# One weight block fewer converted during attention, longer first segments in the first layer, and two changes in the second layer's sums

## The chip, the cores and the metric

The kernel runs on one core of a Trainium2 chip. The metric is the device time of one execution in microseconds, as the median of several runs.

## The reference

Causal attention with a decay (4 batches of 8 heads, 576 positions, 64 per head), and behind it two feed-forward layers on 2304 tokens of 512 elements:

```python
log_f = np.log(np.clip(f, 0.0001, 1.0))
cum = np.cumsum(log_f, axis=-1)
scores = scale * q @ k.T + (cum[:, :, :, None] - cum[:, :, None, :])   # causal
attn = softmax(scores) @ v                    # -> x [2304, 512]
h = x @ w_in                                  # w_in [512, 2048]
x = (h * np.cos(h)) @ w_out                   # w_out [2048, 512]
g, val = x @ w_gate, x @ w_val                # [512, 1536] each
out = (g / (1 + np.exp(-g)) * val) @ w_out2   # w_out2 [1536, 512]
```

## The kernel before

All weights arrive as 64-bit integers that hold the bits of a double; the kernel turns them into fp32 itself, and makes each fp32 product from a high and a low part, so that one product of a 128-wide block with a chunk of 384 tokens is 12 matmuls of 128x384.

**Weight blocks.** There are 68 blocks of 128x512: 32 of `w_in` and `w_out` of the first layer (called i0 to i15 and o0 to o15 here), 36 of the second layer. `w_load` (L149) loads a raw block through SP into one of two `wraw` buffers. `w_step` converts it in steps: 1 is an Abs on ACT (L165), 2 to 5 are four instructions on DVE (L167 to L173), 6 rounds to the high part (POOL, L115, in attention, ACT, L187, later) and 7 is POOL's subtraction for the low part (L112). Blocks of the second layer go instead to `w_member`: POOL sums (L206), ACT highs, POOL lows, and SP stores to DRAM (L220). The first SA = 16 blocks in the order of a list are converted during attention, with buffers of its own; the rest (the next stage) during the first layer. The list alternates in and out blocks, i0, o0, i1, o1 and so on.

**Attention** runs 16 head pairs through a table of operations (`SCH`, "operation@offset"; w1 to w7 are the steps of a block, wd its load, xo the store of a pair's output x1 to DRAM, L539). `op` and `act` carry them out.

**First layer.** Six chunks of 384 tokens times 16 blocks make 96 steps. A step issues in1 (12 matmuls with w_in, L250, into h), and on ACT n (L661), on DVE r (L663), on ACT the sine (L665), on DVE h (L667), on ACT gh (L669) and on DVE gl (L112); two steps later comes out1 (12 matmuls with w_out, L684; L687 for a segment's last block). Chunks 0 and 1 are cut into two segments each: `SEG` runs blocks 0 to JS - 1 of both, then the rest of both, the sum between being kept in a part in DRAM (L697). ACT, DVE and the others work in the written order; `ORD1` is the order within a step, and each "w" in it may take a substep (2 to 5) of a conversion. `WQ` says how many do:

```python
left = WQ[wpos[0] >= SB and i % 2] if i >= WS else 0     # WQ = (3, 2), SB = 32, WS = 2
```

So three of the four substeps of a block in each step until 32 blocks are done, then three and two in turn. With substep 5 the next block's Abs is issued, and the load of the block after (`w_load(n + RWB2)`). Each later chunk's x is loaded (L264) some steps ahead and split by POOL (xh L115, xl L112). A `gate` (L141) is a one-element write on DVE that holds the load of chunk 1's x until the last pair's attention is done.

**Second layer.** Sums and differences of 2x2 blocks cut eight products to seven. `in2` runs 18 units of seven products (12 matmuls, L872); DVE combines them (L749) in tiles u (six buffers, p1, u2 and u3 of a unit), and silu times value goes to tiles g (two buffers). Three dummy allocations of u ahead of it set which u buffer comes first. `out2` runs 18 sets (t) of products (L961); DVE's sums (`g_sums`) and splits (`g_split`, high on ACT L743, low on DVE L112) of set t + 1 are issued between the products of set t, at places given by `GSUMS` (`GSUM0` for t = 0), `HAT` and `LATG`.

Of the kernel before, what the change touches and what calls it, by code (L numbers as in the profile page):

```python
# [9 lines left out]
F32 = mybir.dt.float32  # L10
# [10 lines left out]
NPAIR = NH // 2  # L21
# [5 lines left out]
CH = 384  # L27
NC = NT // CH
HT = NT // 2
SA = 16  # L30
LAG = 2
PB = 4
RWB = 3
# [10 lines left out]

CPD = ("10", "11")
SCH = "M21@2 ld@0 M00@2 rt@3 M01@2 T40@3 M30@2 T30@3 re@4 C20@3 rc@3 C40@3 C30@3 T10@3 M31@2 w6@4 C10@3 w1@3 T11@3 C11@3 T00@3 C00@3 T01@3 E20@2 C01@3 S4@2 S1@2 V1@4 rf@4 E21@2 w2@3 E30@2 w3@3 w4@3 E31@2 q3@1 M40@2 M10@2 wd@2 E00@2 E01@2 q0@0 M11@2 rd@3 V0@4 S2@1 lv@3 E40@2 S0@1 w5@3 E10@2 xk@3 xo@5 E11@2 q1@0 qb@0 S3@1 T20@2 N1@4 ra@2 N0@4 rb@2 M20@1 w7@4 q2@0"
JS = 8
NCH = 96
NPASS, NQ, NST = 3, 6, 2
NIT = NPASS * CH // 128  # L50
# [1 line left out]
PO = (1, 6, 2, 7, 5, 4, 3)  # L52
PO2 = (1, 5, 6, 2, 7, 3, 4)
HAT = (2, 3, 4, 5, 6, 7, 8)
LAT = (4, 5, 5, 6, 7, 8, 9)
LATG = (3, 4, 5, 6, 7, 8, 9)
# [2 lines left out]
POS_IN = {1: 0, 2: 1, 5: 2, 6: 3, 7: 4, 3: 5, 4: 6}  # L59
POS_OUT = {2: 0, 3: 1, 5: 2, 6: 3, 7: 4, 4: 5, 1: 6}  # L60
GSUMS = ((0, 0), (1, 1), (2, 2), (3, 3))
GSUM0 = ((2, 0), (3, 1), (4, 2), (6, 3))
SEAM = {1: (2, 3), 6: (3, 4), 5: (4, 5), 2: (5, 6), 7: (6, 7), 3: (7, 8), 4: (8, 9)}
ORD1 = "0c152cw64cowwc"
WQ = (3, 2)
NS = 2
WS = 2
# [27 lines left out]
def body(ctx: ExitStack, tc: tile.TileContext, qk, v, f, w_in, w_out, w_gate, w_val, w_out2, mask_c, ident_c, sel_c, out):  # L95
# [24 lines left out]
    SB = 2 * J1  # L120
    srcs = {"i": w_in, "o": w_out, "g": w_gate, "v": w_val, "p": w_out2}
    order = []
    for j in range(SA // 2):
        order += [("i", j), ("o", j)]
# [10 lines left out]
    held, now = [0], [0]  # L135
# [413 lines left out]

    def op(o, i):  # L550

        if not 0 <= i < NPAIR + (o[0] == "w"):
            return
        if i == 0:
            o = {"M40": "M10", "M10": "M11", "M11": "M40"}.get(o, o)
        elif i == 1:
            o = {"S2": "S3", "S0": "S2", "S3": "S0"}.get(o, o)
        if i in (0, 1, NPAIR - 1):
            o = {"rt": "T40", "T40": "T30", "T30": "rt", "rc": "C40", "C40": "C30", "C30": "rc"}.get(o, o)
        if (o, i) in BEHIND:  # L560
            return
        for a in AHEAD.get((o, i), ()):
            act(*a)
        act(o, i)

    AHEAD = {("M21", 1): (("ra", 0), ("rb", 0)), ("M00", 1): (("E20", 1),), ("C40", 0): (("E21", 1),),
             ("w6", NPAIR): [(f"w{k}", NPAIR) for k in range(2, 6)]}
    BEHIND = {a for b in AHEAD.values() for a in b}

    def act(o, i):  # L570
# [129 lines left out]
    wpos = [SA, 2]  # L700
# [27 lines left out]
    def x_tile(b):  # L728
        xid[b], X[b] = slot_tile([128, 2, CH], F32, "xb")
# [34 lines left out]
    for i in range(NCH + LAG):  # L764
        if i < NCH:
            g, j = steps[i]
            c, a, b = SEG[g]
            if j == max(a, b - 5):
                part[g] = pp.tile([128, KD, CH], F32, tag="part", name="part")
                if a:  # L770
                    SP.dma_start(out=part[g], in_=x2[c])
            if j == J1 - 7 and c + 1 not in loaded or c == 0 and j == 2 and 1 not in loaded:
                loaded.add(c + 1)
                load_chunk(c + 1, later=True)
            if i == 0:
                for n in range(RWB2):
                    w_load(SA + n)
            if i == WS:
                w_step(SA, 1)
            left = WQ[wpos[0] >= SB and i % 2] if i >= WS else 0  # L780
            now[0] = i
            for k in ORD1:
                if k in "01234":
                    in1(c, j, int(k))
                elif k in "56" and i:
                    in1(SEG[steps[i - 1][0]][0], steps[i - 1][1], int(k))
                elif k == "w" and left:
                    left -= 1
                    w_next()
                elif k == "o" and i >= LAG:  # L790
                    out1(*steps[i - LAG])
                elif k == "c" and small and small[0][0] <= i:
                    small.pop(0)[1]()
            if xsplit and i >= XS:
                split_x(*xsplit.pop(0))
            if i == NCH - 1:
                in1(c, j, 5)
                in1(c, j, 6)
        else:
            out1(*steps[i - LAG])  # L800
        if i == TCL:
            assert wpos[0] >= len(order) and not small and not xsplit, (wpos, len(small))
            rctx.close()
            cp[0] = ctx.enter_context(tc.tile_pool(name="cmb", bufs=1, side=SIDE_R, reuse_waits="tile"))
        if i >= LAG and steps[i - LAG][0] == last:
            j = steps[i - LAG][1]
            free += [2 * j, 2 * j + 1]
            if j == 1:
                for e in range(4):
                    x_tile(e)  # L810
                    x_read(e, 0)
            elif j == 3:
                for e in range(4, 7):
                    x_tile(e)
                jobs += [(u, k) for u in range(4) for k in PO]
            while jobs and free:
                u_read(*jobs.pop(0))
        if TCL < i <= TCL + 4:
            x_sums()[i - TCL - 1]()
        if TCL < i <= TCL + 7:  # L820
            x_split(PO[i - TCL - 1], 0)
            x_split(PO[i - TCL - 1], 1)
# [4 lines left out]
    wk = ctx.enter_context(tc.tile_pool(name="wk", bufs=1, reuse_waits="tile"))  # L827
    ps = ctx.enter_context(tc.tile_pool(name="ps", bufs=1, space=PSUM, reuse_waits="tile"))
    for t in "cd":
        ps.tile([128, 2, 512], F32, tag=t, name=t)  # L830
    for _ in range(3):
        wk.tile([128, 2, CH], F32, tag="u", name="u", bufs=6)

    def parts(i):
        return ((0, 0), (1, 0), (0, 1))
# [19 lines left out]
    def in2(p, q, after, final):  # L855

        pa, pb = (ps.tile([128, 2, 512], F32, tag=t, name=t) for t in "ab")
        ct = ps.tile([128, 2, 512], F32, tag="c", name="c")
        a, b, c = (t[:, :, :CH] for t in (pa, pb, ct))
        acc = {1: (a, 1, 0), 2: (a, 0, 1), 6: (b, 1, 0), 7: (b, 0, 0), 4: (b, 0, 1), 5: (c, 1, 0), 3: (c, 0, 1)}  # L860
        p1, u2, u3 = (wk.tile([128, 2, CH], F32, tag="u", name=n, bufs=6) for n in ("p1", "u2", "u3"))
        g = wk.tile([128, 4, CH], F32, tag="g", name="g", bufs=2)
        for i in PO:
            o, s, e = acc[i]
            for mem in range(2):
                n = 0
                for x, y in ((0, 0), (1, 0), (0, 1)):
                    for kt in range(2):
                        d, r = o[:, mem], cmb[i][:, y, kt]
                        if final and not mem and n == 0 and i in (5, 6):  # L870
                            d, r = (ct if i == 5 else pb)[:, 0], cmb[i][:, 0].rearrange("p k t -> p (k t)")[:, :512]
                        PE.matmul(d, lhsT=wu[q, i][1][:, mem, x, 128 * kt:128 * kt + 128], rhs=r,  # L872
                                  start=bool(s and n == 0), stop=(n == 5), skip_group_check=True)
                        n += 1
            if i == 1:
                ACT.copy(out=p1, in_=a)
            elif i == 6:
                tt(u2, b, p1, add)
            elif i == 2:
                silu(DVE, a, g, p, q, 0)  # L880
            elif i == 7:
                tt(u3, b, p1, add)
            elif i == 5:
                tt(u3, c, u3, add)
                if final:
                    at(3, silu, DVE, u3, g, p, q, 3)
                else:
                    silu(POOL, u3, g, p, q, 3)
            elif i == 4:
                tt(p1, b, p1, add)  # L890
                if final:
                    at(3, silu, DVE, p1, g, p, q, 2)
                else:
                    silu(POOL, p1, g, p, q, 2)
            else:
                tt(u2, c, u2, add)
                at(1, silu, POOL, u2, g, p, q, 1)
            after(i)
# [14 lines left out]
    def g_split(t, i, k):  # L913
        g = [x[1] for x in GT[t]]
        s1, s2, s4 = (sums[e][1] for e in range(3))
        (low_c if k else high_c)(i, {1: g[0], 6: s2, 2: g[2], 7: g[1], 5: s1, 4: g[3], 3: s4}[i])
        if i == 4 and k:
            free.extend(x[0] for x in GT.pop(t))
# [67 lines left out]
        while jobs and len(free) > n:  # L986
            u_read(*jobs.pop(0))

    def splits(fn, lat, po=PO):
        for i, h, d in zip(po, HAT, lat):  # L990
            at(h, fn, i, 0)
            at(d, fn, i, 1)

# [14 lines left out]
    for st in range(NST):  # L1008
        for p in range(NPASS):
            final = st == NST - 1 and p == NPASS - 1  # L1010
            for q in range(NQS * st, NQS * st + NQS):
                k = q - NQS * st
# [23 lines left out]
    for t in range(NIT):  # L1036
        if t + 1 < NIT:
            for d, n in GSUMS if t else GSUM0:
                at(d, g_sums, t + 1, n)
            splits(lambda i, k, t=t: g_split(t + 1, i, k), LATG, PO2)  # L1040
        if t + 2 < NIT:
            at(2, g_load, t + 2)
        out2(t, lambda i: step())
# [58 lines left out]
```

## Time and profile before

| | us |
|---|---|
| median of 3 runs | 976.17 (974.88 to 976.98) |
| profiled execution | 975.54 |
| its span in the trace | 973.8 |
| PE busy | 963.0 (99% of the span) |
| DVE, ACT, POOL busy | 730.8, 506.0, 465.3 |
| mean granted TensorE clock | 0.998 |

The span runs from the first to the last instruction; the profiled execution is 1.74 us longer. Times within the trace are counted from the span's start.

### The profile page before, as it was taken

Reading aid. Unit: us, or ns where it says so; the run is one execution under the profiler, and the core shown is the slowest. Engines: PE = TensorE matmul, PEld = TensorE weight load, DVE = VectorE, ACT = ScalarE, POOL = GpSimd, SP = SyncE. Lnnn points to the kernel's source line nnn. Section 1 sums busy time; section 2 is a strip of 40 time slices with the busy share of each in tenths; the row PEclk is TensorE's granted clock in tenths of the full one; section 3 lists DMA queues with packets and bytes.
Section 4 is the critical chain, followed back from the end, with each engine's and each line's share of the span. In section 5 each row is a group of like instructions: output and inputs, shape, how many; then the busy total and the mean of one; then the engine's idle time right before and its main releaser. Section 6 shows DMA issues by size and latency. Waiting matters only on the chain.

```text
span 973.8 us, 17222 instructions
## 1 busy us (share of the span) xinstructions
PE 963.0 (99%) x6106; PEld 909.3 (93%) x6106; DVE 730.8 (75%) x1309; ACT 506.0 (52%) x1106; POOL 465.3 (48%) x494
## 2 busy tenths in 40 slices
PE   8999999999999999999999999999999999999998
PEld 5778787899999999999999999999999999888888
DVE  6988887787788877779775635766768585898884
ACT  7888887465545655646555432323224132454552
POOL 7787875332257678686582005445445455100000
PEclk9999999999999999999999999999999999999999
DMA  6666656333467868768757773325941329953431
GB/s 190 213 214 193 218 171 190 131 119 108 152 195 250 248 195 285 223 215 283 248 186 244 254 267 109 113 68 200 334 129 51 114 63 382 353 179 126 135 108 44
DMA packets 108981, 182.55 MB, mean 187 GB/s; under 512 B 8912, under 2 KB 72800, under 8 KB 108896
## 3 DMA queue, kind: packets, MB, share of 16 engines
q1 hardware_dynamic: 108896, 181.46, 57.2%
q8 instruction: 48, 0.79, 0.3%
q14 instruction: 37, 0.30, 0.1%
HBM read 118.43 MB, written 62.99 MB: 186 GB/s over the span
## 4 chain that ended last, share of the span: by engine, by line
PE 92%; DMA 3%; ACT 2%; DVE 2%; issue 1%; POOL 0%; DVEq 0%; ACTq 0%; POOLq 0%; SPq 0%
PE h L250 19%; PE t L684 18%; PE b L872 11%; PE c L872 8%; PE a L872 7%; PE b L961 5%; PE t L525 4%; PE t L474 4%; PE a L961 3%; PE sB L405 2%; PE c L961 2%; PE d L961 2%; PE t L687 2%; PE sA L405 2%; PE sA L413 2%; DMA wraw<-in_w_in_dram 1%
## 5 line engine op out<-in xcount | busy, mean ns | idle before, releaser
L250 PE MATMUL h<-xh,w 128*128 128x384 f32 x768 | 148.9, 334 | 0.0
L684 PE MATMUL t<-gh,w 128*128 128x384 f32 x704 | 138.4, 338 | 3.1 <-ACT gh L669 3.0
L250 PEld LDWEIGHTS h<-xh,w 128*128 128x128 f32 x768 | 134.4, 188 | 0.2 <-issue 0.2
L840 POOL TENSOR_TENSOR s<-u,s 128x384 f32<-128x384 f32 x35 | 39.7, 1136 | 190.6 <-ACT s L839 184.1
L684 PEld LDWEIGHTS t<-gh,w 128*128 128x128 f32 x704 | 124.0, 189 | 4.9 <-ACT gh L669 4.0
L872 PE MATMUL b<-c,wu 128*128 128x384 f32 x648 | 121.3, 334 | 0.3 <-DVE u L749 0.3
L663 DVE SCALAR_TENSOR_TENSOR r<-h,n 128x384 f32<-128x384 f32 x96 | 53.3, 555 | 89.6 <-ACT n L661 89.0
L872 PEld LDWEIGHTS b<-c,wu 128*128 128x128 f32 x648 | 113.0, 188 | 0.7 <-DVE u L749 0.6
L661 ACT ACTIVATE n<-h 128x384 int32<-128x384 f32 x96 | 47.1, 490 | 119.3 <-PE h L250 119.0
L250 PE MATMUL h<-xl,w 128*128 128x384 f32 x384 | 82.3, 334 | 0.0
L872 PE MATMUL c<-c,wu 128*128 128x384 f32 x432 | 80.7, 334 | 0.0
L872 PE MATMUL a<-c,wu 128*128 128x384 f32 x432 | 80.7, 334 | 0.0
L684 PE MATMUL t<-gl,w 128*128 128x384 f32 x352 | 75.5, 335 | 0.0
L872 PEld LDWEIGHTS c<-c,wu 128*128 128x128 f32 x432 | 75.4, 188 | 0.0
L872 PEld LDWEIGHTS a<-c,wu 128*128 128x128 f32 x432 | 75.4, 188 | 0.0
L112 POOL TENSOR_TENSOR w<-ta,w 128x512 fp32r<-128x512 f32 x32 | 45.1, 1409 | 56.2 <-ACT w L187 28.3
L436 ACT ACTIVATE P<-P,mx 128x384 f32<-128x384 f32 (+3 forms) x128 | 70.3, 550 | 1.3 <-DVE mx L428 1.2
L250 PEld LDWEIGHTS h<-xl,w 128*128 128x128 f32 x384 | 67.9, 188 | 0.2 <-issue 0.2
L173 DVE SCALAR_TENSOR_TENSOR ta<-wraw,ta 128x512 int32<-128x512 int32 x68 | 66.4, 976 | 0.5
L665 ACT ACTIVATE r<-r,hpi 128x384 f32<-128x384 f32 x96 | 59.6, 620 | 12.7 <-DVE r L663 12.0
L165 ACT ACTIVATE ta<-wraw 128x512 f32<-128x512 f32 x68 | 46.2, 679 | 38.2 <-DMA wraw<-in_w_out_dram 13.1
L684 PEld LDWEIGHTS t<-gl,w 128*128 128x128 f32 x352 | 62.8, 189 | 0.0
(148 smaller groups left out, 2066.6 us busy)
## 6 DMA issues: line engine op xcount, KB each, us to landing
wu<-wu SPq DMA_DIRECT2D x63, 512.0 KB, 4.5
wraw<-in_w_out_dram SPq DMA_DIRECT2D x28, 512.0 KB, 4.2
wu<-hi SPq DMA_DIRECT2D x54, 256.0 KB, 3.9
gd<-g SPq DMA_DIRECT2D x72, 192.0 KB, 2.3
gt<-gd SPq DMA_DIRECT2D x36, 384.0 KB, 4.6
raw<-in_qk_dram SPq DMA_DIRECT2D x16, 576.0 KB, 5.3
wu<-sums SPq DMA_DIRECT2D x36, 256.0 KB, 4.6
xb<-x SPq DMA_DIRECT2D x24, 384.0 KB, 7.6
```

Source lines behind the costliest of these rows:

```text
L112: eng.tensor_tensor(out=o, in0=a, in1=b.bitcast(F32), op=ALU.subtract)
L165: ACT.activation(out=ta.bitcast(F32), in_=hi32, func=AF.Abs)
L173: DVE.scalar_tensor_tensor(out=ta, in0=hi, scalar=-(1 << 30), in1=ta, op0=ALU.bitwise_and, op1=ALU.bitwise_or)
L250: PE.matmul(ps, lhsT=w[:, a, 128 * kk:128 * kk + 128], rhs=b[:, kk], start=(n == 0), stop=(n == 3 * KD - 1))
L436: ACT.activation(out=o, in_=o, func=AF.Exp, scale=-1.0, bias=mxt[p % 8][:, t:t + 1], accum_out=smt[p // 2 % 3][:, c:c + 1])
L661: ACT.activation(out=n, in_=h, func=AF.Copy, scale=INV2PI, bias=0.25)
L663: DVE.scalar_tensor_tensor(out=r, in0=h, scalar=INV2PI, in1=n, op0=ALU.mult, op1=ALU.subtract)
L665: ACT.activation(out=r, in_=r, func=AF.Sin, bias=hpi, scale=float(2 * np.pi))
L684: PE.matmul(acc[m][:, :CH], lhsT=wo[:, q, 128 * m:128 * m + 128], rhs=x, start=(j == a and n == 0), stop=False)
L840: e.tensor_tensor(out=s, in0=C[:, 0], in1=s, op=ALU.mult)
L872: PE.matmul(d, lhsT=wu[q, i][1][:, mem, x, 128 * kt:128 * kt + 128], rhs=r, start=bool(s and n == 0), stop=(n == 5), skip_group_check=True)
L961: PE.matmul(ot[:, :w], lhsT=cmb[i][:, x, q], rhs=m[:, 256 * y:256 * y + w], start=(i in (1, 5) and n == 0), stop=(n == len(ops) - 1), skip ...
```

## The change

Four things. SA becomes 15: the attention's table converts one block less, so the extra w operations behind the last pair go, and the list runs ..., i7, and then i8, o7, i9, o8 and on. JS becomes 9: the first segments of chunks 0 and 1 have nine blocks, the second ones seven. The last 12 blocks are converted at three substeps a step again. In the second layer the first unit's u2 and u3 share one g buffer, the dummy allocations go, and in out2 the sums and splits that are issued with t = 0 come one product later.

```diff
--- before.py
+++ after.py
@@ -27,7 +27,7 @@
 CH = 384
 NC = NT // CH
 HT = NT // 2
-SA = 16
+SA = 15
 LAG = 2
 PB = 4
 RWB = 3
@@ -44,7 +44,7 @@
 
...
-JS = 8
+JS = 9
 NCH = 96
 NPASS, NQ, NST = 3, 6, 2
 NIT = NPASS * CH // 128
@@ -59,7 +59,8 @@
 POS_IN = {1: 0, 2: 1, 5: 2, 6: 3, 7: 4, 3: 5, 4: 6}
 POS_OUT = {2: 0, 3: 1, 5: 2, 6: 3, 7: 4, 4: 5, 1: 6}
 GSUMS = ((0, 0), (1, 1), (2, 2), (3, 3))
-GSUM0 = ((2, 0), (3, 1), (4, 2), (6, 3))
+GSUM0 = ((3, 0), (4, 1), (5, 2), (6, 3))
+HAT0, LAT0 = (3, 4, 5, 6, 7, 8, 8), (4, 5, 6, 7, 8, 9, 9)
 SEAM = {1: (2, 3), 6: (3, 4), 5: (4, 5), 2: (5, 6), 7: (6, 7), 3: (7, 8), 4: (8, 9)}
 ORD1 = "0c152cw64cowwc"
 WQ = (3, 2)
@@ -549,7 +550,7 @@
 
     def op(o, i):
 
-        if not 0 <= i < NPAIR + (o[0] == "w"):
+        if not 0 <= i < NPAIR:
             return
         if i == 0:
             o = {"M40": "M10", "M10": "M11", "M11": "M40"}.get(o, o)
@@ -563,8 +564,7 @@
             act(*a)
         act(o, i)
 
-    AHEAD = {("M21", 1): (("ra", 0), ("rb", 0)), ("M00", 1): (("E20", 1),), ("C40", 0): (("E21", 1),),
-             ("w6", NPAIR): [(f"w{k}", NPAIR) for k in range(2, 6)]}
+    AHEAD = {("M21", 1): (("ra", 0), ("rb", 0)), ("M00", 1): (("E20", 1),), ("C40", 0): (("E21", 1),)}
     BEHIND = {a for b in AHEAD.values() for a in b}
 
     def act(o, i):
@@ -777,7 +777,7 @@
                     w_load(SA + n)
             if i == WS:
                 w_step(SA, 1)
-            left = WQ[wpos[0] >= SB and i % 2] if i >= WS else 0
+            left = WQ[SB <= wpos[0] < SB + 24 and i % 2] if i >= WS else 0
             now[0] = i
             for k in ORD1:
                 if k in "01234":
@@ -828,8 +828,6 @@
     ps = ctx.enter_context(tc.tile_pool(name="ps", bufs=1, space=PSUM, reuse_waits="tile"))
     for t in "cd":
         ps.tile([128, 2, 512], F32, tag=t, name=t)
-    for _ in range(3):
-        wk.tile([128, 2, CH], F32, tag="u", name="u", bufs=6)
 
     def parts(i):
         return ((0, 0), (1, 0), (0, 1))
@@ -858,7 +856,12 @@
         ct = ps.tile([128, 2, 512], F32, tag="c", name="c")
         a, b, c = (t[:, :, :CH] for t in (pa, pb, ct))
         acc = {1: (a, 1, 0), 2: (a, 0, 1), 6: (b, 1, 0), 7: (b, 0, 0), 4: (b, 0, 1), 5: (c, 1, 0), 3: (c, 0, 1)}
-        p1, u2, u3 = (wk.tile([128, 2, CH], F32, tag="u", name=n, bufs=6) for n in ("p1", "u2", "u3"))
+        p1 = wk.tile([128, 2, CH], F32, tag="u", name="p1", bufs=6)
+        if now[0]:
+            u2, u3 = (wk.tile([128, 2, CH], F32, tag="u", name=n, bufs=6) for n in ("u2", "u3"))
+        else:
+            u = wk.tile([128, 4, CH], F32, tag="g", name="g", bufs=2)
+            u2, u3 = u[:, :2], u[:, 2:]
         g = wk.tile([128, 4, CH], F32, tag="g", name="g", bufs=2)
         for i in PO:
             o, s, e = acc[i]
@@ -986,8 +989,8 @@
         while jobs and len(free) > n:
             u_read(*jobs.pop(0))
 
-    def splits(fn, lat, po=PO):
-        for i, h, d in zip(po, HAT, lat):
+    def splits(fn, lat, po=PO, hat=HAT):
+        for i, h, d in zip(po, hat, lat):
             at(h, fn, i, 0)
             at(d, fn, i, 1)
 
@@ -1037,7 +1040,7 @@
         if t + 1 < NIT:
             for d, n in GSUMS if t else GSUM0:
                 at(d, g_sums, t + 1, n)
-            splits(lambda i, k, t=t: g_split(t + 1, i, k), LATG, PO2)
+            splits(lambda i, k, t=t: g_split(t + 1, i, k), *((LATG, PO2) if t else (LAT0, PO2, HAT0)))
         if t + 2 < NIT:
             at(2, g_load, t + 2)
         out2(t, lambda i: step())
```

SP, at the end of attention (x1 stores of the last pairs, raw loads wraw, and xl, the load of chunk 1's x). Before:

```order
L539 DMA x1_60<-xp_2574 128x576
L539 DMA x1_60<-xp_2602 128x576
L149 DMA wraw_2642<-in_w_in_dram 128x512
L149 DMA wraw_2644<-in_w_in_dram 128x512
L264 DMA xl_2687<-x1_60 128x4x384
```

And in the changed kernel:

```order
L540 DMA x1_60<-xp_2572 128x576
L150 DMA wraw_2631<-in_w_in_dram 128x512
L150 DMA wraw_2633<-in_w_out_dram 128x512
L540 DMA x1_60<-xp_2598 128x576
L265 DMA xl_2676<-x1_60 128x4x384
```

The two raw loads moved ahead of the last x1 store.

POOL, at the same place (w13, w14 and so on are blocks, rounded and then subtracted; xh and xl the splits of a chunk). Before:

```order
L112 TENSOR_TENSOR w13_2519<-ta_2405,w13_2519 128x512
L115 TENSOR_SCALAR w14_2580<-ta_2522 128x512
L112 TENSOR_TENSOR w14_2580<-ta_2522,w14_2580 128x512
L115 TENSOR_SCALAR w15_2610<-ta_2582 128x512
L112 TENSOR_TENSOR w15_2610<-ta_2582,w15_2610 128x512
L115 TENSOR_SCALAR xh_2688<-xl_2687 128x384
L112 TENSOR_TENSOR xl_2687<-xl_2687,xh_2688 128x384
```

And in the changed kernel:

```order
L113 TENSOR_TENSOR w13_2519<-ta_2405,w13_2519 128x512
L116 TENSOR_SCALAR w14_2578<-ta_2522 128x512
L113 TENSOR_TENSOR w14_2578<-ta_2522,w14_2578 128x512
L116 TENSOR_SCALAR xh_2677<-xl_2676 128x384
L113 TENSOR_TENSOR xl_2676<-xl_2676,xh_2677 128x384
```

The pair for w15 is gone from here, and the subtraction of w14 is the last of the attention's blocks.

DVE, in out2 with t = 0 (g and u the results of this set, gs and gt sums for the next set, c their low parts). Before:

```order
L749 TENSOR_TENSOR g_9515<-a_9511,g_9515 128x256
L749 TENSOR_TENSOR gt0_9171<-gt31_9170,gt0_9171 128x768
L112 TENSOR_TENSOR c1_9579<-gt31_9170,c1_9579 128x768
L749 TENSOR_TENSOR u_9619<-b_9512,u_9516 128x512
L749 TENSOR_TENSOR g_9515<-u_9619 128x256
```

And in the changed kernel:

```order
L749 TENSOR_TENSOR g_9511<-a_9507,g_9511 128x256
L749 TENSOR_TENSOR gs28_9163<-gt0_9167,gt2_9169 128x768
L749 TENSOR_TENSOR u_9611<-b_9508,u_9512 128x512
L749 TENSOR_TENSOR g_9511<-u_9611 128x256
L749 TENSOR_TENSOR gt0_9167<-gt31_9166,gt0_9167 128x768
L113 TENSOR_TENSOR c1_9597<-gt31_9166,c1_9597 128x768
```

u and the g that is made of it moved ahead of gt0 and of the low part c1.

## Rows read from the trace of the kernel before

**Rows 1.** The page, part 1: busy time, share and instructions of each engine.

```profile
PE 963.0 (99%) x6106; PEld 909.3 (93%) x6106; DVE 730.8 (75%) x1309; ACT 506.0 (52%) x1106; POOL 465.3 (48%) x494
```

**Rows 2.** Waits of PE: line and releaser, us in total, times, longest.

```profile
PE t L684 <- ACT gh L669: 3.0, 3, 2.3
...
PE b L961 <- DVE u L749: 0.4, 1, 0.4
```

**Rows 3.** Chain at the end of attention: start, duration (us), what.

```profile
176.19 3.71 DMA wraw<-in_w_in_dram
...
185.35 2.08 PE h L250 x12
```

**Rows 4.** Timeline there: start, us, engine, line, instruction, idle before.

```profile
168.75 1.28 POOL L112 TENSOR_TENSOR w<-ta,w 128x512 fp32r<-128x512 f32 x1
...
176.93 1.55 PE L250 MATMUL h<-xh,w 128*128 128x384 f32 x8
...
181.44 2.93 PE L684 MATMUL t<-gh,w 128*128 128x384 f32 x8 [2.27 <-ACT gh L669]
...
185.19 1.55 PE L250 MATMUL h<-xh,w 128*128 128x384 f32 x8
```

**Rows 5.** Windows, PE alone: length, busy (instructions), granted clock, DMA share, GB/s.

```profile
179.20:181.40 2.20, 0.00 (x0) 1.00 0.95 345
181.40:183.00 1.60, 1.56 (x5) 0.52 0.87 325
```

**Rows 6.** DMA issues: engine, operation, count, KB each, median us to landing.

```profile
x<-xp SPq DMA_DIRECT2D x16, 288.0 KB, 2.1
```

**Rows 7.** Timeline of the first steps of the first layer.

```profile
202.80 1.29 POOL L112 TENSOR_TENSOR w<-ta,w 128x512 fp32r<-128x512 f32 x1 [1.29 <-ACT w L187]
```

**Rows 8.** Timeline from the first to the second layer.

```profile
574.19 2.24 PE L872 MATMUL a<-c,wu 128*128 128x384 f32 x12
...
579.84 0.96 DVE L749 TENSOR_TENSOR u<-b,p 128x768 f32<-128x768 f32 x1 [4.89 <-DMA x<-part]
...
583.07 2.24 PE L872 MATMUL c<-c,wu 128*128 128x384 f32 x12
```

**Rows 9.** Timeline of the second unit's g.

```profile
593.98 1.02 POOL L841 TENSOR_TENSOR g<-u,s 128x384 f32<-128x384 f32 x1
...
596.87 0.56 DVE L841 TENSOR_TENSOR g<-a,s 128x384 f32<-128x384 f32 x1
```

**Rows 10.** Timeline of out2, t = 0.

```profile
847.54 2.26 PE L961 MATMUL c<-wu,c 128*128 128x512 f32 x12
...
852.43 0.86 PE L961 MATMUL a<-wu,c 128*128 128x512 f32 x3
```

**Rows 11.** Windows of out2: length, busy of PE, PEld, DVE, ACT, POOL, clock, DMA.

```profile
855.00:955.00 100.00, 100.00 (x573) 87.76 (x572) 87.59 (x119) 52.27 (x82) 0.00 (x0) 1.00 0.41 129
```

**Rows 12.** Timeline where chunk 3's x meets the conversions.

```profile
350.18 0.51 POOL L115 TENSOR_SCALAR xh<-xl 128x384 fp32r<-128x384 f32 x1 [4.77 <-DMA xl<-x]
...
369.78 0.67 ACT L165 ACTIVATE ta<-wraw 128x512 f32<-128x512 f32 x1 [5.31 <-DMA wraw<-in_w_val_dram]
```

**Rows 13.** Timeline of PE, where groups start at these two places.

```profile
368.56 1.55 PE L250 MATMUL h<-xh,w 128*128 128x384 f32 x8
...
384.06 1.55 PE L684 MATMUL t<-gh,w 128*128 128x384 f32 x8
...
436.06 1.55 PE L250 MATMUL h<-xh,w 128*128 128x384 f32 x8
...
449.39 1.55 PE L250 MATMUL h<-xh,w 128*128 128x384 f32 x8
```

**Rows 14.** Windows of the first layer, columns as in the windows of out2.

```profile
181.00:270.00 89.00, 88.56 (x502) 88.56 (x503) 72.76 (x136) 50.85 (x102) 30.93 (x24) 0.98 0.38 124
...
475.00:520.00 45.00, 45.00 (x262) 45.00 (x261) 32.35 (x56) 25.03 (x54) 33.91 (x34) 1.00 0.68 220
```

**Rows 15.** L173 from 300 to 500 us: ns min/median/max, first and last start.

```profile
L173 DVE SCALAR_TENSOR_TENSOR ta<-wraw,ta x29: 674/682/1669, 306.9 to 494.3; 128x512 int32<-128x512 int32 x29
```

## Prediction

> **What bounds the kernel now.** The page comes first: PE is busy 963.0 us of a span of 973.8 us, 99%, and no other engine passes 75% [rows 1]. So the end moves only by what PE loses: 10.8 us stand idle, and stretches at a lower clock add to that. The waits of PE are then read: ACT's gh (L669) holds it three times, 3.0 us in all, the longest 2.3 us, and DVE's u (L749) once in the last part, 0.4 us [rows 2]. The rest of the waits lies in the attention, in products that the change leaves in their order. Then the chain of waits and the timeline are read around each of these places. What PE loses at one is the start of a later product less the start of an earlier one, less 2.08 us for each group of twelve matmuls between them, so that slow groups count too. (Twelve matmuls take 2.08 us where nothing disturbs them [rows 3], a step of the first layer two such groups, 4.16 us.)
>
> **Seam 1, attention to first layer.** Two weight loads start at 176.19 us, when POOL has done its subtraction for the 16th block, whose buffer they need; they land 3.71 us later, at 179.90 us, and Abs, n and gh follow on ACT, so that PE starts at 181.44 us after 2.27 us of waiting [rows 3, 4]. The granted clock was still 1.00 while the engine stood idle, and 0.52 behind the gap: TensorE ran at 1.2 in place of 2.4 GHz [rows 5]. Together: the product of step 3 starts at 185.19 us; two groups after 176.93 us would be 176.93 + 2 x 2.08 = 181.09 us. **The place costs 4.10 us**, more than the waits' table shows.
>
> With 15 blocks converted in attention, the raw load of the first block of the next stage waits for the 15th block's subtraction, which ended at 168.75 + 1.28 = 170.03 us [rows 4]: 6.1 us earlier. The loads land at about 170.05 + 3.71 = 173.8 us. PE wants gh at 176.93 + 2.08 = 179.01 us, and from the landing to PE's start 181.44 - 179.90 = 1.54 us went by, so a landing behind 177.5 us would cost something. That leaves 3.7 us of cover; if it is gone, all 4.10 us come back.
>
> What is late next: the x1 store of the last pair now stands on SP behind the two weight loads, and DVE's gate (L141) writes where the attention's last output lay, so that it waits for that store, and h and gh stand behind it. If that store moves only when both loads have landed, and then takes the 2.1 us that an x1 store takes in the median from issue to landing [rows 6], the gate opens at 173.8 + 2.1 = 175.9 us. With the same 1.54 us for h and gh behind it that is about 177.4 us, against 179.0 us. I take the seam as gone, -4.10 us; the bounds are -4.10 and 0.
>
> Four blocks now must be ready that were not among the first: i8, o7, i9 and o8. The fourth block of this stage was subtracted by 202.80 + 1.29 = 204.09 us before [rows 7], so by about 200.0 us now. The in1 of step 3 started at 185.19 us [rows 4], the out1 of step 2 one group later, and the out1 of step 8 six steps of 4.16 us behind that, at 212.2 us; now 4.1 us earlier, at 208.1 us: 8 us to spare. That a segment is nine blocks long rather than eight moves one x2 store by a step, and no wait of PE stands there. Zero.
>
> **Seam 2, first to second layer.** DVE's u waits 4.89 us for the store of the part, since it writes where the part was, and PE behind it starts late. Its fifth group begins at 583.07 us [rows 8], where 574.19 + 4 x 2.08 = 582.51 us was due: **0.56 us**. In a g buffer, u2 waits for no store, and only for PE's product. What it may cost: the second unit's g now takes the buffer that POOL reads last for the first unit, ending at 593.98 + 1.02 = 595.00 us; DVE writes that g at 596.87 us [rows 9], 1.9 us later. Zero, and up to the full 0.56 us back if this cover goes. I take -0.56 us.
>
> **Seam 3, first product set of the last part.** DVE's u comes behind gt and c low, and PE waits 0.4 us for it [rows 2]; its next product but one starts at 852.43 us where 847.54 + 2 x 2.10 = 851.74 us was due [rows 10]: **0.69 us**. (2.10 us for a group here, as it reads 2.26 us where one of the layer before reads 2.24 us [rows 8].) In the new order u stands ahead of gt and c low. An instruction of 768 columns takes 0.96 us on DVE [rows 8], so u comes up to 1.9 us sooner, against 0.4 us of wait. The sums and splits move one product later, and DVE in the 100 us behind is busy 87.59 us [rows 11], so 12 us are left to make that up. -0.69 us; bounds -0.69 and +0.7 (the same wait one product later).
>
> **The middle of the first layer.** At two places a chunk's load meets the conversions. POOL waits 4.77 us for the x [rows 12] and then splits it, with sums between; SP's stores of the sums, which come late, queue in front of the next raw load; the Abs of that block waits 5.31 us [rows 12], and PE for gh behind it. From 368.56 to 384.06 us stand seven groups, 14.56 us, so 0.94 us are lost; from 436.06 to 449.39 us six, 12.48 us, so 0.85 us [rows 13]. **Together 1.79 us.** The two waits for gh left over in the table are 3.0 - 2.3 = 0.7 us [rows 2], some 0.4 us at each, so that an Abs that waits less than about 5.31 - 0.4 = 4.9 us costs PE nothing.
>
> Now the conversions come one block, that is 1.6 steps of 4.16 us at 2.5 of 4 substeps a step, later against these loads, and POOL's order shows the four splits of the fourth chunk spread over sums, where before two pairs stood together. Worked through by hand with the durations of [rows 12], the longest wait of an Abs there becomes some 3.3 us: no loss. In the last chunk loaded, where the last 12 blocks run at three substeps a step again, I get about 4 us, close to the 4.9. I take one such place as left, +0.9 us; bounds 0 and 1.8 us (two).
>
> **The pace of the last 12 blocks.** They take 16 steps in place of 19.2. Where three substeps a step ran before, DVE was busy 72.76 of 89 us, or 3.40 of the 4.16 us of a step; where 2.5 ran late in the layer, 32.35 of 45 us [rows 14]. PE lost nothing in either beyond the seam's end. But in the first of these stretches POOL worked 30.93 of 89 us, in the second 33.91 of 45 us, and beside POOL's sums DVE is slower: from 300 us on L173 takes 674 ns at the least and 1669 ns at the most [rows 14, 15]. The Trainium skill (SBUF — State Buffer, Who interferes with whom) says that a VectorE instruction with two SBUF inputs and a GpSimd instruction take turns under an exclusive lock, so that one waits for the other's whole instruction. The maximum above agrees with it, but the median is 682 ns [rows 15], near the least, so it is seldom met; met in each step it would make the last rival below true. By the rows I take zero.
>
> **The sum.** On the profiled run of 975.54 us: 975.54 - 4.10 - 0.56 - 0.69 - 1.79 + 0.9 = 969.3 us. The median of the runs, 976.17 us, stands 0.63 us above the profiled run, so 969.9 us is what the median should be.
>
> **The rivals.**
> *The middle gets worse.* The faster pace makes the Abs of the last chunk wait longer, and two to four more places of 0.9 us appear. For it: every place in this layer has only some tenths of cover, and SP's queue is in order. Against it: 475 to 520 us shows no loss with POOL at 75%. Time: 969.9 + 0.9 x 2 to 0.9 x 4 = 971.7 to 973.5 us, say 972.6 us.
> *The wait of seam 1 only moves.* The change does not do there what it says: the last x1 store comes too late for the gate, or the loads wait for something else. For it: that store now stands behind two loads of half a megabyte each, and the DMA engines were 95% busy between 179.2 and 181.4 us [rows 5]. Against it: 1.6 us to spare by the sum above. As the clock fell after one gap of 2.2 us, an equal gap gives the 4.10 us back: 974.0 us, up to 974.9 us with no gain in the middle.
> *Slower.* With the last 12 blocks at three a step, DVE becomes the bound. Its 3.40 us, times 1.1 for longer instructions, are 3.74 us, and 0.42 us are left. If one instruction in each step is held for a whole POOL subtraction of 1.29 us [rows 7], that is 5.03 us, 0.87 us too long, over 16 steps 13.9 us: 969.9 + 13.9 = 983.8 us. It is slower than before from 6.3 us over 16 steps, 0.4 us a step. Against it: 181 to 270 us ran at this pace with no such loss.
>
> **How the numbers follow.** The forecast has 0.54 (its own range 968.6 to 971.2 us, from the bounds of the middle and seam 3), the worse middle 0.17, the moved wait 0.14, slower 0.07, and 0.08 is for what goes better, down to 968.4 us (the middle gone whole gives 969.0 us, and 968.4 us if the next median stands no higher than this profiled run). The range 968.4 to 973.6 us leaves out most of the moved wait and the slow case. What can be told from no change is about 0.2%, 1.95 us: faster is below 974.2 us, slower above 978.1 us. Half of the moved wait and 0.03 of the worse middle fall within that: faster 0.54 + 0.08 + 0.14 + 0.07 = 0.83, same 0.10, slower 0.07.
>
> **What would show it.** In the profile after, PE should wait nowhere for gh at about 180 us and the granted clock stay at 1.00 there; the first wraw loads should issue at 170 us, the Abs start by 177 us. No wait for u should stand at the two later seams, the last part's u starting right behind PE's product b. In the middle one group or none should show 2.3 us. A loss between steps 74 and 80, or PE waits for n or gl there, would be the second or the fourth case, and a clock of 0.5 near 180 us the third.

## The result and the profile after

The changed kernel takes 981.29 us in the median (979.80 to 984.86, six runs), the kernel before 975.58 us: ratio 1.0061, 95% interval 1.0040 to 1.0082. It is slower by 0.6%; 969.9 us was forecast. Its profiled execution took 981.45 us, with a span of 979.7 us. (The runs before the prediction, with a median of 976.17 us, are among the six of before.)

The three seams went as forecast. The timeline of the changed kernel at each of them, columns as in [rows 4]:

```profile
169.29 0.34 SPq L150 DMA_DIRECT2D wraw<-in_w_in_dram  x1
...
174.69 0.65 ACT L166 ACTIVATE ta<-wraw 128x512 f32<-128x512 f32 x1
...
175.14 0.14 DVE L142 CAST xl<-gs 1x1 fp32r<-1x1 f32 x1 [0.54 <-DMA x<-xp]
...
176.96 1.55 PE L251 MATMUL h<-xh,w 128*128 128x384 f32 x8
...
181.12 1.55 PE L251 MATMUL h<-xh,w 128*128 128x384 f32 x8
...
580.12 2.24 PE L875 MATMUL a<-c,wu 128*128 128x384 f32 x12
...
588.44 1.72 PE L875 MATMUL c<-c,wu 128*128 128x384 f32 x9
...
852.83 2.26 PE L964 MATMUL c<-wu,c 128*128 128x512 f32 x12
...
857.03 2.26 PE L964 MATMUL a<-wu,c 128*128 128x512 f32 x12
...
867.53 2.26 PE L964 MATMUL c<-wu,c 128*128 128x512 f32 x12
...
869.99 2.37 PE L964 MATMUL b<-wu,c 128*128 128x512 f32 x12 [0.20 <-DVE u L749]
```

At seam 1 the loads issue at 169.3 us, the gate opens at 175.1 us, and the next in1 starts 4.16 us after that of 176.96 us, where before it took 8.26 us [rows 4]: 4.10 us gained. At seam 2 four groups take 588.44 - 580.12 = 8.32 us, 0.56 us less than 8.88 us [rows 8]. At seam 3 two groups take 4.20 us where they took 4.89 us [rows 10]: 0.69 us. Of that 0.36 us came back one set later, where PE waits for u again (869.99 - 867.53 = 2.46 us for 2.10).

The second layer starts at 580.12 us, 5.93 us later than the 574.19 us of [rows 8], although 4.10 us were gained ahead of it. So the first layer's middle lost **10.0 us more than before**. PE's waits, in the columns of [rows 2], say for whom:

```profile
PE t L684 <- ACT gh L669: 8.5, 4, 3.1
...
PE b L964 <- DVE u L749: 0.2, 1, 0.2
```

The timeline of PE and ACT says where; at each place the last in1 ahead of the loss, the Abs, the product that waits for gh, and an in1 behind it:

```profile
351.76 1.55 PE L251 MATMUL h<-xh,w 128*128 128x384 f32 x8
354.53 0.67 ACT L166 ACTIVATE ta<-wraw 128x512 f32<-128x512 f32 x1 [5.69 <-DMA wraw<-in_w_gate_dram]
355.99 1.67 PE L684 MATMUL t<-gh,w 128*128 128x384 f32 x8 [1.99 <-ACT gh L669]
...
368.35 0.67 ACT L166 ACTIVATE ta<-wraw 128x512 f32<-128x512 f32 x1 [4.79 <-DMA wraw<-in_w_val_dram]
369.81 1.67 PE L684 MATMUL t<-gh,w 128*128 128x384 f32 x8 [1.05 <-ACT gh L669]
372.20 1.56 PE L251 MATMUL h<-xh,w 128*128 128x384 f32 x8
...
422.16 1.55 PE L251 MATMUL h<-xh,w 128*128 128x384 f32 x8
425.30 0.67 ACT L166 ACTIVATE ta<-wraw 128x512 f32<-128x512 f32 x1 [5.55 <-DMA wraw<-in_w_val_dram]
426.77 2.82 PE L684 MATMUL t<-gh,w 128*128 128x384 f32 x8 [2.36 <-ACT gh L669]
430.52 1.55 PE L251 MATMUL h<-xh,w 128*128 128x384 f32 x8
...
501.84 1.55 PE L251 MATMUL h<-xh,w 128*128 128x384 f32 x8
504.92 0.67 ACT L166 ACTIVATE ta<-wraw 128x512 f32<-128x512 f32 x1 [6.73 <-DMA wraw<-in_w_out_dram]
507.15 1.67 PE L684 MATMUL t<-gh,w 128*128 128x384 f32 x8 [3.06 <-ACT gh L669]
509.35 1.55 PE L251 MATMUL h<-xh,w 128*128 128x384 f32 x8
```

There are three places, one for each chunk load in the middle. From 351.76 to 372.20 us stand four steps, 16.64 us, so 3.80 us are lost, in two waits; from 422.16 to 430.52 us one step, 4.20 us lost (4.7 us with the small losses up to 449.8 us); from 501.84 to 509.35 us one step, 3.35 us lost. With these and other small losses the layer loses 12.1 us from 176.96 us on, where before it lost 2.1 us beside the 4.10 us of the seam, 1.79 us of them at the two places of [rows 13].

How the first place comes about is read from the timeline of SP, POOL and DVE:

```profile
338.51 0.49 SPq L265 DMA_DIRECT2D xl<-x  x1
342.62 0.68 DVE L174 SCALAR_TENSOR_TENSOR ta<-wraw,ta 128x512 int32<-128x512 int32 x1
345.43 0.52 POOL L116 TENSOR_SCALAR xh<-xl 128x384 fp32r<-128x384 f32 x1 [5.76 <-DMA xl<-x]
347.00 1.19 POOL L207 TENSOR_TENSOR sums<-ta,sums 128x256 f32<-128x256 f32 x1
348.26 2.31 POOL L113 TENSOR_TENSOR ta<-ta,hi 128x512 f32<-128x512 f32 x2
349.90 0.36 SPq L221 DMA_DIRECT2D wu<-ta  x1
350.36 0.42 SPq L150 DMA_DIRECT2D wraw<-in_w_gate_dram  x1
```

POOL stands 5.76 us in front of a split whose x has not landed. Behind that split, in POOL's order, are the last of a block pair's four sums and its low parts; SP waits for the first low part to store it; and behind that store stands the next raw load. Its buffer was free at 342.62 + 0.68 = 343.30 us; it is issued at 350.36 us, 7.06 us later, and lands 4.2 us after that, when the Abs has waited 5.69 us and PE 1.99 us. In the kernel before the wait for x stood ahead of a pair's first sum [rows 12], and SP waited 6.9 us at the longest for a low part. It is 10.5 us now, as the waits of SP say (us in total, times, longest; first before, then after):

```profile
SPq L220 <- POOL ta L112: 55.6, 29, 6.9
...
SPq L221 <- POOL ta L113: 62.4, 25, 10.5
```

### The profile page after: what moved, and what is told of

Read it like the earlier page. It is cut to its first block, busy times and chain, and to the rows that moved or that the text cites. A ratio compares the mean times of both kernels' runs of the same rounds, so it can differ in the third digit from the quotient of the medians.

```text
span 979.7 us, 17216 instructions
## 1 busy us (share of the span) xinstructions
PE 963.9 (98%) x6106; PEld 909.6 (93%) x6106; DVE 733.8 (75%) x1309; ACT 506.9 (52%) x1107; POOL 466.3 (48%) x493
## 4 chain that ended last, share of the span: by engine, by line
PE 81%; POOL 5%; DMA 5%; DVE 4%; ACT 2%; issue 2%; SPq 0%; POOLq 0%; DVEq 0%; ACTq 0%
PE h L251 14%; PE t L684 12%; PE b L875 11%; PE c L875 8%; PE a L875 8%; PE b L964 5%; PE t L475 4%; PE t L526 4%; PE a L964 3%; DMA xl<-x 2%; PE sB L406 2%; PE sA L406 2%; PE sA L414 2%; PE c L964 2%; PE d L964 2%
## 5 line engine op out<-in xcount | busy, mean ns | idle before, releaser
L174 DVE SCALAR_TENSOR_TENSOR ta<-wraw,ta 128x512 int32<-128x512 int32 x68 | 65.3, 960 | 0.5
L172 DVE SCALAR_TENSOR_TENSOR ta<-wraw,ta 128x512 int32<-128x512 int32 x68 | 63.9, 939 | 1.0
```

Source lines behind the costliest of these rows:

```text
L172: DVE.scalar_tensor_tensor(out=ta, in0=lo, scalar=29, in1=ta, op0=ALU.logical_shift_right, op1=ALU.bitwise_or)
L174: DVE.scalar_tensor_tensor(out=ta, in0=hi, scalar=-(1 << 30), in1=ta, op0=ALU.bitwise_and, op1=ALU.bitwise_or)
```

## The experiments

Theory A: the time at which x lands, against the conversions, decides, by the chain POOL, SP, raw load, Abs, gh. Theory B: the faster pace of the last 12 blocks. Theory C: the DMA engines are full (their share was 1.01 from 355 to 357 us), and the raw loads come late for that. Each was timed in five rounds against the kernel before.

**1. x earlier.** For chunks 3, 4 and 5:

```diff
-            if j == J1 - 7 and c + 1 not in loaded or c == 0 and j == 2 and 1 not in loaded:
+            if j == J1 - (7 if c < 2 else 9) and c + 1 not in loaded or c == 0 and j == 2 and 1 not in loaded:
...
+                hold = i + (0 if c < 2 else 2)
-            if xsplit and i >= XS:
+            if xsplit and i >= max(XS, hold):
```

> The changed kernel, with the x loads of chunks 3, 4 and 5 issued two steps (8.3 us) earlier and POOL's splits left where they are. Theory A (POOL's wait for x): POOL stands up to 6.3 us in front of a split whose load has not landed, with half of a member's sums behind it, and so the stores on SP, the raw load, the Abs and gh come late. Then all three places in the first layer shrink, PE's waits for gh fall from 8.5 us to below 2 us, and the median is 971 to 973 us, below the kernel before (975.6). Theory B (pace of the last 12 blocks): only the first two places shrink, the third (3.35 us) stays, about 975 us. Theory C (DMA engines full): the raw loads land late because the engines are busy, an earlier x load does not help, 979 us or more.

973.14 us, ratio 0.9978 (0.9962 to 0.9994). POOL waits for x nowhere there, the first two places lose 0.7 us together. Against C as it was put, an earlier x was enough; but the x load's own traffic moved with it, and experiment 2 leaves that where it was. At the third place one wait for gh of 2.24 us is left, and the place loses 2.6 us, with no wait for x; so a part of B stands. This is the timeline of that place:

```profile
485.43 0.76 DVE L174 SCALAR_TENSOR_TENSOR ta<-wraw,ta 128x512 int32<-128x512 int32 x1
489.41 0.36 SPq L221 DMA_DIRECT2D wu<-ta  x1
490.19 0.34 SPq L150 DMA_DIRECT2D wraw<-in_w_out_dram  x1
495.38 0.66 ACT L166 ACTIVATE ta<-wraw 128x512 f32<-128x512 f32 x1 [5.05 <-DMA wraw<-in_w_out_dram]
497.76 1.68 PE L685 MATMUL t<-gh,w 128*128 128x384 f32 x8 [2.24 <-ACT gh L670]
```

and its windows, with POOL's busy time in the third number:

```profile
484.00:497.00 13.00, 12.75 (x14) 1.00 0.70 217
```

The raw load is again behind the store, 4.0 us after its buffer was free (486.19 us), but POOL is late because it works all the time, 12.75 of 13 us.

**2. The splits later.** The loads stay where they are, and the splits wait:

```diff
+                hold = i + (0 if c < 2 else 2)
-            if xsplit and i >= XS:
+            if xsplit and i >= max(XS, hold):
```

> The changed kernel, with the x loads where they are and POOL's splits of chunks 3, 4 and 5 taken up two steps later. Theory A: POOL finds the load landed, so its waits of 6 us go as well, and the time is that of the earlier load within 2 us (971 to 974 us). Theory C: no change, 979 us or more. Theory D (the splits' own time on POOL, 6 us for four, at this phase of the sums, and not the wait): a loss stays in another place, 976 to 980 us.

970.37 us, ratio 0.9943 (0.9923 to 0.9963): 0.5% below before. PE's wait for gh is 0.2 us in all, the fast pace is still there, and 475 to 520 us shows PE busy 45.00 of 45 us. C and D fall with it, as the loads keep their place in the order. Where B's part went is not told by this run: the splits stand elsewhere against the sums, too.

**3. x earlier in the kernel before**, the edit of experiment 1.

> The kernel before with the x loads of chunks 3, 4 and 5 issued two steps earlier. Theory A: its two places (0.94 and 0.85 us) go, POOL's wait of 4.77 us too, about 973.7 us against 975.6 us. Theory C: no change.

973.48 us, ratio 0.9976 (0.9963 to 0.9990). As theory A had it: 2.0 us less, for the 1.79 us of [rows 13].

**4. The second layer's edits alone**, in the kernel before (that part of the diff above).

> The kernel before with the edits of the second layer alone (u2 and u3 of the first unit in a g buffer, no dummy allocations, the sums and splits for t = 1 one product later). By the prediction's terms 0.56 + 0.69 = 1.25 us less: 974.3 us. Rival: the groups of out2 that read 2.12 us in place of 2.10 us in the changed kernel's profile come with these edits, 0.02 us for each of some 45 groups, and 0.4 us return behind t = 1: about 975.5 us, no change.

974.22 us, ratio 0.9985 (0.9969 to 1.0002). 1.3 us less where 1.25 us was expected, at the edge of what can be told from none.

**5. The pace.** Two runs: the changed kernel with the edit below, and the kernel before with the fast pace of the last 12 blocks alone (that one line of the change).

```diff
-            left = WQ[SB <= wpos[0] < SB + 24 and i % 2] if i >= WS else 0
+            left = WQ[SB <= wpos[0] < SB + 32 and i % 2] if i >= WS else 0
```

> The changed kernel with the faster pace for the last 4 blocks only, in place of the last 12. Theory B (pace): with the faster pace POOL is busy 36.3 of 45 us in the third place and the raw load waits behind its stores, so the loss of 3.35 us there shrinks to about 1 us, and the other two places stay: about 979 us. Theory A alone (the wait for x): the third place stays as well, 981 us.

> The kernel before with the faster pace of the last 12 blocks alone. Theory B: a third place of 2 to 3.4 us appears in the last chunk, 977.5 to 979 us against 975.5. Theory A (it takes the shifted phase too): no change, 975.5 us within 1 us.

981.47 us, ratio 1.0062 (1.0043 to 1.0081), and 974.65 us, ratio 0.9993 (0.9977 to 1.0009). By itself the pace costs nothing that can be told, neither way. At the slower pace POOL stood 6.15 us in front of the third place's first split, and the loss there did not shrink. The row puts the end of that wait down to PE's in1; but the split began 7.6 us behind the issue of its x load, as the three of the changed kernel did (6.9 to 7.6 us), so I take it for the same wait for x.

**6. Both: x earlier and the slower tail.**

> Early x loads and the faster pace for the last 4 blocks only. Early loads alone left one wait for gh of 2.2 us in the third place, without a wait of POOL for x. Theory B for that rest: it goes, 970 to 971 us against 973.1 us. If the rest is not from the pace: 973 us.

969.59 us, ratio 0.9947 (0.9929 to 0.9965), the lowest of all. What experiment 1 left at the third place is gone, so there the pace does count, once the wait for x is out of the way: it fills POOL while the four splits are to be done.

**7. Splits later and the slower tail.**

> Splits two steps later, and the faster pace for the last 4 blocks only. The two steps together: the first gave 970.4 us with no wait for x left, the second took 3.5 us from the early loads but nothing from the changed kernel. If only the waits counted, 970 us, as with the first alone; if the tail still costs something, 969 us.

971.14 us, ratio 0.9961 (0.9950 to 0.9973). Not told apart from experiment 2.

**8. Load and splits together, later.**

```diff
-            if j == J1 - 7 and c + 1 not in loaded or c == 0 and j == 2 and 1 not in loaded:
+            if j == J1 - (7 if c < 2 else 5) and c + 1 not in loaded or c == 0 and j == 2 and 1 not in loaded:
```

> The changed kernel with load and splits of chunks 3, 4 and 5 both two steps later, so that they meet the conversions about as before, and POOL still waits 5 us for x. Theory A in its narrow form (the wait costs only where it stands in the middle of a block pair's sums): the first two places shrink from 3.8 and 4.8 us to about 0.9 us each, 973 to 976 us. In its wide form (any such wait of POOL costs as much): 980 us. Rival: the splits are now too late for the chunk's first steps, PE waits for xh, over 981 us.

981.63 us, ratio 1.0062 (1.0043 to 1.0081). The waits of PE name the rival:

```profile
PE t L684 <- ACT gh L669: 4.6, 1, 4.6
PE h L251 <- POOL xh L116: 4.4, 2, 2.2
```

The splits came too late for the chunk's first products, so this run tells nothing on the phase.

**9. Load and splits together, earlier**: by two steps in the kernel before (7 becomes 9 in that line), and by one step in the changed kernel (8).

> The kernel before with load and splits of chunks 3, 4 and 5 both two steps earlier. Nothing of the change is in it; only the phase is new: POOL's first split of each chunk now stands behind the third of a block pair's four sums, where the changed kernel has it, instead of ahead of a pair. Theory A in its narrow form (the phase is all): it loses at three places as the changed kernel does, some 10 us, 983 to 987 us against 975.5. If the other parts of the change were needed for the loss, or only a late x mattered: 974 to 977 us.

> The changed kernel with load and splits of chunks 3, 4 and 5 both one step earlier: for chunks 3 and 4 the first split stands ahead of a pair's sums again, for chunk 5 still behind the third sum, and POOL still waits 4 to 6 us for x each time. Narrow form of A: the first two places lose about 0.9 us each in place of 3.8 and 4.8, the third stays, about 974 to 975.5 us. Wide form (the wait costs wherever it stands): 980 us or more.

976.69 us, ratio 1.0016 (0.9998 to 1.0034), and 980.80 us, ratio 1.0067 (1.0053 to 1.0080). The narrow form of A falls with the first. Its timeline has the order of the changed kernel and nearly the same wait of POOL, but little loss:

```profile
343.03 0.51 POOL L115 TENSOR_SCALAR xh<-xl 128x384 fp32r<-128x384 f32 x1 [6.02 <-DMA xl<-x]
...
352.06 0.67 ACT L165 ACTIVATE ta<-wraw 128x512 f32<-128x512 f32 x1 [4.15 <-DMA wraw<-in_w_gate_dram]
...
355.44 1.67 PE L684 MATMUL t<-gh,w 128*128 128x384 f32 x8 [0.17 <-ACT gh L669]
```

The raw load lands 1.5 us sooner against ACT than in the changed kernel (a wait of the Abs of 4.15 us for 5.69), and PE waits 0.17 us for 1.99. So some 4.0 us of this Abs wait were covered, and 3.7 us of that in the changed kernel. Why the Abs waits 1.5 us less behind the same wait of POOL was not taken apart. The second run shows the same from the other side: its first two places lose 1.3 and 2.6 us in place of 3.8 and 4.7 us, its third 8 us. A shift only moves the loss about.

**10. SP's stores behind the raw load.** In the changed kernel POOL's low parts are stored a step later:

```diff
-            put(i, 1, source(i))
+            late.append((now[0] + 1, lambda t=source(i): put(i, 1, t)))
...
+        while late and late[0][0] <= i:
+            late.pop(0)[1]()
```

> The changed kernel with SP's stores of POOL's low parts put a step later in the order, so that the next raw load stands ahead of the store that it waited behind (7 us at the first place). If SP's queue is the link between POOL's wait and the Abs: waits for gh fall from 8.5 to below 3 us, 973 to 976 us, while POOL still waits about 6 us for x. If the link is another (POOL or DVE themselves late, or the DMA engines full): 980 us.

974.07 us, ratio 0.9992 (0.9983 to 1.0001). SP is the link: with its order changed, and POOL's left as it was, the first place's loss is gone. In its timeline POOL waits for x as long as ever, and the raw load no longer cares:

```profile
341.74 0.68 DVE L175 SCALAR_TENSOR_TENSOR ta<-wraw,ta 128x512 int32<-128x512 int32 x1
342.45 0.35 SPq L151 DMA_DIRECT2D wraw<-in_w_gate_dram  x1
344.66 0.51 POOL L116 TENSOR_SCALAR xh<-xl 128x384 fp32r<-128x384 f32 x1 [5.87 <-DMA xl<-x]
347.98 0.66 ACT L167 ACTIVATE ta<-wraw 128x512 f32<-128x512 f32 x1
```

It is issued 0.03 us after its buffer came free, not 7.06 us, and the Abs waits for nothing. What is left, some 3.7 us, lies at the second place, where PE waits for ACT. The third place loses 0.5 us, although POOL stands 5.3 us in front of the first split there and is then busy 12.7 of the 13 us from 484 us on, with the fast pace still in: both causes of that place's loss go through SP's order. The chain's other half is POOL's order: the Trainium skill (Perfetto Trace Analysis, Tensor Engine Instruction (MATMUL, LD_WEIGHTS)) says that ACT, DVE and GpSimd take their instructions strictly first in, first out. The trace agrees: in the changed kernel the last sum of a block pair, whose block DVE had finished at 343.30 us, started 1.6 us behind the split's start of 345.43 us, and no instruction of POOL ran in the 5.76 us ahead of it.

**11. The time of x alone.** The x load of chunks 3 to 5 is issued ahead of the raw load that it stood behind, and the splits are held where they were:

```diff
         if k == 5 and n + RWB2 < len(order):
+            if xnext[0]:
+                loaded.add(xnext[0])
+                load_chunk(xnext[0], later=True)
...
             w_load(n + RWB2)
```

> The changed kernel with one row moved on SP three times: the x load stands ahead of the raw load (and two stores) that it stood behind. At the first two places it is issued 2.3 to 2.4 us earlier, at the third 0.4 us; the order of POOL, ACT and DVE is that of the changed kernel. If the loss follows the time at which x lands (each us of Abs wait beyond 3.7 us costs PE one): POOL's wait falls to 3.4 and 3.9 us, the Abs waits of 5.7 and 5.55 us to about 3.3 us, the first two places lose under 1 us each in place of 3.8 and 4.8, the third keeps 3.35: 973 to 975 us. If the order of the queues is what costs: 980 us or more.

975.71 us, ratio 1.0000 (0.9989 to 1.0012), a little above what was expected. The x load no longer waits with the raw load for its buffer, and so comes more than the 2.4 us earlier:

```profile
333.04 0.46 SPq L265 DMA_DIRECT2D xl<-x  x1
339.52 0.51 POOL L116 TENSOR_SCALAR xh<-xl 128x384 fp32r<-128x384 f32 x1 [0.54 <-DMA xl<-x]
343.77 0.35 SPq L150 DMA_DIRECT2D wraw<-in_w_gate_dram  x1
347.99 0.68 ACT L166 ACTIVATE ta<-wraw 128x512 f32<-128x512 f32 x1 [0.62 <-DMA wraw<-in_w_gate_dram]
```

With POOL, ACT and DVE in the order of the changed kernel, the first two places lose 0.5 us together. The third lost more than expected, 6.1 us, with a wait for x of 1.5 us only; POOL is busy there 12.76 of the 13 us from 484 to 497 us, nearly the 12.75 us of experiment 1. Of the 6.1 us, 2.9 us are groups behind the wait, at a granted clock of 0.58.

**12. What the attention's edit is worth**: the kernel before with experiments 1 and 4 together.

> The kernel before with the edits of the second layer and the early x loads, without the change in attention: what is left between it and the changed kernel with early loads and a slow tail (969.6 us) is what the attention's edit itself is worth. By the prediction's terms 975.5 - 1.25 - 1.8 = 972.4 us, so about 3 us for the attention's edit (4.10 us predicted). If the edit is worth nothing: 969.6 us.

973.12 us, ratio 0.9978 (0.9965 to 0.9991). Against experiment 6 (ratio 0.9947) that leaves 0.31%, 3.0 us, or 3.5 us by the medians, for the edit in attention with its longer segments. 4.10 us was the term. The two profiles say where the rest is: the seam costs 4.1 us in this run, but experiment 6 still loses 1.0 us in the middle, and this run nothing.

## Why the prediction was wrong

**Right:** the seams. The terms of 4.10, 0.56 and 0.69 us are in the profile after as large as forecast, the last with 0.36 us given back a set later, so that it is worth 0.33 us. The covers held: the gate opened at 175.1 us where 175.9 was reckoned, and the loads came at 169.3 us. No rival at seam 1 came true, and the pace of the last 12 blocks did not make DVE the bound: alone it changed nothing that can be told in the kernel before (experiment 5). One reading behind that was wrong: the median of 682 ns for L173 [rows 15] was taken to say that its lock is seldom met. In that trace 14 of the 29 instructions took 0.84 to 1.67 us, each of them beside one of POOL's; even so DVE was not the bound.

One reservation holds for the 4.10 us. It was read from one execution, in which the granted clock fell behind the wait. In the profile of the kernel before with the fast tail alone (experiment 5), whose attention is the same, PE waits as long and the clock stays at 1.00; the place costs 182.75 - 176.14 - 4.16 = 2.45 us:

```profile
176.14 1.55 PE L250 MATMUL h<-xh,w 128*128 128x384 f32 x8
...
180.53 1.68 PE L684 MATMUL t<-gh,w 128*128 128x384 f32 x8 [2.15 <-ACT gh L669]
...
182.75 1.55 PE L250 MATMUL h<-xh,w 128*128 128x384 f32 x8
```

So about 1.65 us of the term is there in some executions of the same code and not in others.

**Wrong:** the step on the middle of the first layer, "the longest wait of an Abs there becomes some 3.3 us: no loss", and with it "one such place as left, +0.9 us". The waits became 5.69, 5.55 and 6.73 us. The order of the four splits was read as relief, since they stood apart; but spread over the sums they hold a pair's sums and low parts behind the wait for x, and SP's store and the raw load behind those. The term of -1.79 + 0.9 us should have been +10.0 us: 975.54 - 4.10 - 0.56 - 0.69 + 10.0 = 980.2 us, where the profiled execution took 981.45 us. (Of the rest 0.36 us are the wait behind seam 3, and about 0.9 us the slower groups of out2 that the last section tells of.)

The second error is in the cover: "an Abs that waits less than about 5.31 - 0.4 = 4.9 us costs PE nothing". In the changed kernel waits of 4.79, 5.69 and 6.73 us cost PE 1.05, 1.99 and 3.06 us: 3.7 us were covered each time, and what lay beyond counted one for one. At the second place 5.55 us cost 2.36 us, so only 3.2 us were covered; in experiment 1 5.05 us cost 2.24 us, a cover of 2.8 us. The 4.9 us held at the places from which it was read, and not elsewhere. That it depends on where the Abs stands within its step is likely, and not shown.

The rival "the middle gets worse" named the place of the loss, but not its cause (it had the faster pace) and not its size: each place cost 3.4 to 4.7 us, not 0.9. With the price taken from places that were only just uncovered, every case but the last ended at or below 974.9 us. The last, "slower", came near with 983.8 us, but by another mechanism, an instruction held in each of 16 steps, which the waits do not show. So the side was missed by a price: that of a wait of which more than expected lay beyond a cover smaller than expected.

What stays open: how much of the third place's loss in the changed kernel is the wait for x (2.65 us there) and how much POOL's full work at the fast pace; experiments 1, 5 and 6 show that both count, not their shares, and experiment 10 that both reach PE through SP's order. In experiment 11, with a wait for x of 1.5 us, it still lost 6.1 us, 2.9 us of them to the clock.

## What to carry to other kernels

When a change shifts one periodic stream against another, look for what the two share: here POOL, which takes splits and sums in one order, and SP, which takes stores and loads in one order, turned a late x into a late weight. Put a wait where nothing needed sooner stands behind it, or start the load early enough that there is none: a load two steps earlier, or splits two steps later, brought 8 to 11 us. A cover that was read at one place isn't a constant: here it was 4.9 us at one place and 2.8 to 4.0 us at the others given above, and what lay beyond it counted in full.

## What the runs showed that was not expected

The granted clock fell after one wait and not after others. In the changed kernel's profile PE waited 1.99, 1.05 and 3.06 us for gh with a granted clock of 1.00 behind each, but after the 2.36 us of the second place it was 0.53, the lower of its two levels. The windows of PE there, columns as in [rows 5]:

```profile
426.70:430.00 3.30, 3.23 (x10) 0.53 1.02 320
```

and behind the longest wait:

```profile
507.10:510.00 2.90, 2.85 (x16) 1.00 0.31 105
```

So the second place lost 4.20 us for a wait of 2.36 us, the third 3.35 us for one of 3.06 us. In the second run of experiment 9 the clock was 0.59 in the 3.4 us behind a wait of only 1.78 us. Nor does the same code do the same each time, as the seam above showed. Of the 92 executions of the kernel before that were timed beside the experiments, 29 have a mean granted clock of 1.000, and in each of the four sets of runs their median is 1.3 to 2.7 us below that of the executions at 0.998; experiment 1 took 970.71 to 971.21 us in three executions at 1.000 and 975.03 to 976.48 us in three at 0.996. A loss that was read behind a wait in one profile can therefore be some 1.7 us off for the next execution. No run here says what decides it.

In out2 a group takes 2.10 us in one profile and 2.12 us in another, all through the set: 2.10 us in the kernel before and experiments 1, 3, 4, 5, 7, 8 and 10, 2.12 us in the changed kernel and experiments 2, 6, 11 and 12 (experiment 9 has one of each), though 4 and 12 have the same second layer. Over some 45 groups that is 0.9 us. No run here says what makes it.
